# Attention by clusters, then a feed-forward block: routing two jobs ahead, maxima one job ahead

## The chip, the cores and the metric

The kernel runs on one core of a Trainium2 chip. The metric is the device time of one execution in microseconds (us). TensorE is PE in the profile (PEld is its weight load), VectorE is DVE, ScalarE is ACT, GpSimd is POOL, and SyncE, which issues all DMAs here, is SP.

## The reference

Queries, keys and values have 4 batches, 8 heads, 768 rows and 64 columns. Each query and each key goes to the nearest of 16 centroids of its head, and a query sees only the keys of its own centroid. The result feeds a block with two weight matrices.

```python
q_assign = argmax(q_n @ c_n.T)          # (B, H, S), 16 clusters; k_assign likewise
mask = q_assign[..., :, None] == k_assign[..., None, :]
scores = where(mask, (q @ k.T) / sqrt(64), -1e9)
attn = softmax(scores)                  # row maximum taken off first
x = (attn @ v) -> (3072, 512)           # heads side by side
h = x @ w_in                            # 512 x 2048
g = h * erf(log(1 + exp(h)))
out = g @ w_out                         # 2048 x 512
```

The weights arrive as 64-bit floats.

## The kernel before, in words

**Jobs.** Heads are taken in pairs, 16 pairs in all, 4 to a batch. A job is a pair and the query halves (384 columns each) that it computes. Jobs 0 to 3 take the first half of pairs 0 to 3, jobs 4 to 7 the second half, and jobs 8 to 19 both halves of pairs 4 to 15. A job has 6 units for each half: in a unit, `scores(u)` writes one key block against one half of both heads into PSUM (`sc`, lines 388 and 394), and ACT takes the exponent (`pr`, line 399). POOL adds the exponents up in `acc` (lines 403 and 407). `attend` multiplies them with the values (`av`, line 418), sums `acc` over the rows (`psum`, line 425), takes the reciprocal (`den`, line 430) and writes `xT` (line 439).

**What a job needs first.** `route(i)` transposes the query and key halves (`pt`, line 255), copies them to `qT` and `kT` (lines 262 and 264) and, crosswise, to the bf16 operands `qm` and `km` (lines 268 and 270), multiplies with the centroids (`psim`, line 276), copies to `sims` (line 283), transposes back (line 287), finds the nearest centroid (`mx`, `sims`, `mr`, `aq`, `ak`, lines 294 to 311), and transposes the one-hot masks (`pb`, line 321) into `qm` and `km` (lines 330 and 332). `shift(i)` then multiplies masks (`sm`, line 346) and lets DVE take the row maxima (`nmx`, line 350). They are joined (`nm`, line 355), transposed (`pn`, line 360), copied (`nmT`, line 362), written to DRAM (`line`, line 364) and read back as one row of `qm` (line 367). The second matmul of each score (line 394) needs that row.

`aside(i + 1)` runs `route` and then `shift` of the next job, one step of it in each slot of the current job; a job with one half has 24 slots, one with two halves 30. So one chain of work for one job runs beside the scores of the job before.

**Beside it.** `convert()` turns the 32 weight pieces from 64-bit to 32-bit floats, with two buffers: `fetch` (line 161), two ACT steps (lines 178 and 179), DVE steps on lines 180, 189, 194 and 197, POOL on line 200 and DVE's finish on line 166. `ffn_stream()` is the feed-forward block, cut into 12 chunks of 256 rows: `hidden` (`hp`, line 479), its copy (`g`, line 486), `gate` (lines 458 to 462) and `project` (`po`, line 500, and `osb`, line 507). `pump` hands out its matmuls by a budget in each slot. A chunk can start when `attend` has finished its rows in all four pairs of the batch.

**Buffers.** `qT`, `kT`, `qm` and `km` have two buffers each, the loaded `in_q` and `in_k` one. All of `pt`, `psim`, `pb`, `pn` and `psum` share a single PSUM buffer (pool `ps_t`). `sc` and `sm` share two (`ps_s`), `hp` and `po` two (`ps_f`), and `av` has one.

**Order.** The text above is not the order on the engines. A scheduler takes the recorded instructions, with their dependences and their buffers, and fixes a sequence for each engine when the program is built; each engine then runs its own sequence in order, waiting on semaphores.

Of the kernel before, what the change touches and what calls it, by code (L numbers as in the profile page):

```python
# [8 lines left out]
F32 = mybir.dt.float32  # L9
# [38 lines left out]
def kernel(  # L48
# [15 lines left out]
    const = pool("const", 1)  # L64
    stage = pool("stage", 1)
    vp = pool("vp", 2)
    rowp = pool("rowp", 2)
    routep = pool("routep", 1)
# [4 lines left out]
    gp = pool("gp", 2)  # L73
    outp = pool("outp", 2)
    setup = pool("setup", 1)
    linep = pool("linep", 2, space=bass.MemoryType.DRAM)
# [20 lines left out]

    def load(i, nm, src, pl, js=range(NJ)):
        if i >= len(JOBS):
            return  # L100
        p = JOBS[i][0]
        b, h0 = p // HP, 2 * (p % HP)
        t = pl.tile([P, NJ, 2, D], F32, name="in_" + nm)
        for e in range(2):
            nc.sync.dma_start(
                out=t[:, js[0] : js[-1] + 1, e],
                in_=src[b, h0 + e].rearrange("(p j) d -> p j d", p=P)[:, js[0] : js[-1] + 1],
            )
        work.setdefault(i, {})[nm] = t

    def chunks(i):

        halves = JOBS[i][1]
        return range(halves[0] * HJ, (halves[-1] + 1) * HJ)

    def load_qk(i):
        if i < len(JOBS):
            load(i, "q", q, stage, chunks(i))
            load(i, "k", k, stage)

    cen = setup.tile([P, D], F32, name="cen")
    nc.sync.dma_start(out=cen, in_=centroids.rearrange("h c d -> (h c) d"))
    load_qk(0)

# [81 lines left out]

    cn = setup.tile([P, 2, D], F32, name="cn")
    sq = cn[:, 0]
    ss = setup.tile([P, 1], F32, name="ss")
    nc.vector.tensor_tensor(out=sq, in0=cen, in1=cen, op=ALU.mult)  # L210
    nc.vector.reduce_sum(out=ss, in_=sq, axis=AX.X)
    nc.vector.tensor_scalar_max(out=ss, in0=ss, scalar1=1e-30)
    norm = setup.tile([P, 1], F32, name="norm0")
    nc.scalar.sqrt(norm, ss)
    for it in range(2):
        inv = setup.tile([P, 1], F32, name=f"inv{it}")
        nc.vector.reciprocal(out=inv, in_=norm)
        twice = setup.tile([P, 1], F32, name=f"twice{it}")
        nc.vector.scalar_tensor_tensor(
            out=twice, in0=ss, scalar=inv, in1=norm, op0=ALU.mult, op1=ALU.add  # L220
        )
        norm = setup.tile([P, 1], F32, name=f"norm{it + 1}")
        nc.vector.tensor_scalar(
            out=norm, in0=twice, scalar1=0.5, scalar2=(1e-6 if it else 0.0),
            op0=ALU.mult, op1=ALU.add,
        )
    rden = setup.tile([P, 1], F32, name="rden")
    nc.vector.reciprocal(out=rden, in_=norm)
# [15 lines left out]
    def route(i):  # L244
        p, halves = JOBS[i]
        st = work[i]
        parts = [("q", h) for h in halves] + [("k", h) for h in range(2)]
        for nm in "qk":
            st[nm + "T"] = rowp.tile([P, S], F32, name=nm + "T")

            st[nm + "m"] = rowp.tile([P, 2, S], BF16, name=nm + "m")
        for nm, half in parts:
            pt = ps_t.tile([P, HJ, P], F32, name="pt", tag="t")
            for jj in range(HJ):
                nc.tensor.transpose(  # L255
                    out=pt[:, jj], in_=st[nm][:, HJ * half + jj].rearrange("p e d -> p (e d)"),
                    identity=ident,
                )
            cols = slice(half * HW, (half + 1) * HW)
            raw = st[nm + "T"][:, cols]  # L260
            if nm == "q":
                nc.scalar.mul(out=raw, in_=pt.rearrange("p j t -> p (j t)"), mul=D**-0.5)
            else:
                nc.scalar.copy(out=raw, in_=pt.rearrange("p j t -> p (j t)"))
            for e in range(2):
                dst = st[nm + "m"][(1 - e) * D : (2 - e) * D, e, cols]
                if nm == "q":
                    nc.gpsimd.tensor_copy(out=dst, in_=raw[e * D : (e + 1) * D])
                else:
                    nc.scalar.copy(out=dst, in_=raw[e * D : (e + 1) * D])  # L270
            yield
        del st["q"], st["k"]
        load_qk(i + 1)
        psim = ps_t.tile([P, HW], F32, name="psim", tag="t")
        for g, (nm, half) in enumerate(parts):
            nc.tensor.matmul(  # L276
                psim[2 * C * g : 2 * C * (g + 1)], lhsT=ccT[:, p % HP],
                rhs=st[nm + "T"][:, half * HW : (half + 1) * HW],
                start=True, stop=True,
            )  # L280
        n = 2 * len(parts)
        sims = routep.tile([P, HW], F32, name="sims")
# [34 lines left out]

        for nm, src, js in (("qm", aq, chunks(i)), ("km", ak, range(NJ))):
            pb = ps_t.tile([P, NJ, P], BF16, name="pb", tag="t")
            for j in js:  # L320
                nc.tensor.transpose(  # L321
                    out=pb[:, j], in_=src[:, j % HJ, j // HJ].rearrange("p e c -> p (e c)"),
                    identity=identb,
                )
            cols = slice(js[0] * P, (js[-1] + 1) * P)
            for e in range(2):
                r = slice(e * D, (e + 1) * D)
                src = pb[r].rearrange("p j t -> p (j t)")[:, cols]
                if nm == "qm":
                    nc.vector.tensor_scalar_mul(out=st[nm][r, e, cols], in0=src, scalar1=-BIG)  # L330
                else:
                    nc.scalar.copy(out=st[nm][r, e, cols], in_=src)  # L332
            yield
# [3 lines left out]
    def shift(i):  # L337
        st = work[i]
        ts = chunks(i)
        n = len(ts)  # L340
        nmx = small.tile([P, NJ, 2, 2], F32, name="nmx")
        for t in ts:
            for half in range(2):
                sm = ps_s.tile([P, 2, 512], F32, name="sm", tag="s")
                for e in range(2):
                    nc.tensor.matmul(  # L346
                        sm[:, e, 0:HW], lhsT=st["qm"][:, e, t * P : (t + 1) * P],
                        rhs=st["km"][:, e, half * HW : (half + 1) * HW], start=True, stop=True,
                    )
# [14 lines left out]
        nc.sync.dma_start(out=line[0 : 2 * n], in_=nmT[0 : 2 * n])  # L364
        for e in range(2):
            r = e * D + SH
            nc.sync.dma_start(
                out=st["qm"][r : r + 1, e, ts[0] * P : (ts[-1] + 1) * P],
                in_=line[e * n : (e + 1) * n].rearrange("(o t) p -> o (t p)", o=1),
            )  # L370
        load(i, "v", v, vp)
        yield

# [7 lines left out]
    def scores(u):  # L381
        i, half, j = units[u]
        st = work[i]
        sc = ps_s.tile([P, 2, 512], F32, name="sc", tag="s")
        cols = slice(half * HW, (half + 1) * HW)
        for e in range(2):
            r = slice(e * D, (e + 1) * D)
            nc.tensor.matmul(  # L388
                sc[:, e, 0:HW], lhsT=st["kT"][r, j * P : (j + 1) * P], rhs=st["qT"][r, cols],
                start=True, stop=False,  # L390
            )
        for e in range(2):
            r = slice(e * D, (e + 1) * D)
            nc.tensor.matmul(  # L394
                sc[:, e, 0:HW], lhsT=st["km"][r, e, j * P : (j + 1) * P], rhs=st["qm"][r, e, cols],
                start=False, stop=True,
            )
# [13 lines left out]
    def attend(u0):  # L411
# [12 lines left out]
        for e in range(2):  # L424
            nc.tensor.matmul(  # L425
                psum[e * D : (e + 1) * D], lhsT=ones, rhs=st["acc", half][:, e], start=True, stop=True
            )
        den = routep.tile([P, HW], F32, name="den")
        nc.scalar.activation(out=den, in_=psum, func=ACT.Identity, bias=alleps)  # L429
        nc.vector.reciprocal(out=den, in_=den)  # L430
        x = xTs.setdefault(p, {})
        lo = half * HW
        while lo < (half + 1) * HW:
            c = lo // TB
            hi = min((c + 1) * TB, (half + 1) * HW)
            if c not in x:
                x[c] = xTp.tile([P, TB], F32, name=f"xT{c}", bufs=XBUFS[c])
            own = slice(lo - half * HW, hi - half * HW)
            nc.vector.scalar_tensor_tensor(  # L439
                out=x[c][:, lo - c * TB : hi - c * TB], in0=av[:, own], scalar=av[:, HW : HW + 1],  # L440
                in1=den[:, own], op0=ALU.add, op1=ALU.mult,
            )
# [103 lines left out]

    def aside(i):

        if i < len(JOBS):
            yield from route(i)  # L550
            yield from shift(i)

    conv = convert()
# [8 lines left out]

    for _ in aside(0):
        prepare(20)
    chunk_cost = NFT * HP * 4 * TB + TJ * NFT * 4 * DM
    ahead = iter(())
    for u in range(0, len(units), 2):
        i, half, j = units[u]
        p, halves = JOBS[i]
        if (half, j) == (halves[0], 0):  # L570
            ahead = aside(i + 1)
        scores(u)
# [8 lines left out]
        slots = SLOTS if len(halves) == 2 else 8  # L581
        for _ in range(slots):
            if part:
                pump(part * chunk_cost // (periods * slots) + 64)
            prepare(4 if i < HP else 6)
            next(ahead, None)
    attend(len(units) - NJ)
# [34 lines left out]
```

## Time and profile before

| | |
|---|---|
| runs | 1381.64, 1381.69 and 1383.28 us, median 1381.69 |
| profiled execution | 1381.38 us, of which its span is 1379.6 us (1.8 us lie around it) |
| granted TensorE clock, mean of the span | 0.956 |
| busy | PE 1265.8 us (92%), DVE 619.0 (45%), ACT 519.5 (38%), POOL 375.6 (27%) |
| first exponent of job 0 | at 47.32 us |
| jobs 0 to 3 | 47.32 to 197.21 us |
| jobs 4 to 7 | 197.21 to 347.31 us |
| jobs 8 to 19 | 347.31 to 1186.12 us |
| feed-forward block alone | 1186.12 to the end |

Job boundaries are put at the first exponent of each job. In rows of the profile "x" gives a count, the first number after the bar is busy time in us, the next the mean of one in ns, and what follows the second bar is idle time of the engine just before, with the engine and line that ended it.

### The profile page before, as it was taken

What the parts mean: (1) busy time and instruction counts of PE and PEld (TensorE: products, weight loads), DVE (VectorE), ACT (ScalarE), POOL (GpSimd) and SP (SyncE); (2) the same over time, 40 slices, a digit from 0 to 9 for tenths busy, and PEclk for the clock granted to TensorE, in tenths of its full rate; (3) what the DMA queues carried; (4) which work ended last, traced back from release to release, by engine and by line L of the source; (5) the groups of instructions that cost most, each with busy time, mean ns of one, the idle gap of its engine ahead of it and who ended that gap; (6) DMA issues with size and microseconds to landing.
All of it is one profiled execution on the core that took longest, in us unless ns stands there. A gap on an engine that the chain in (4) does not pass through costs nothing.

```text
span 1379.6 us, 13584 instructions
## 1 busy us (share of the span) xinstructions
PE 1265.8 (92%) x5393; PEld 667.9 (48%) x5393; DVE 619.0 (45%) x859; ACT 519.5 (38%) x645; POOL 375.6 (27%) x293
## 2 busy tenths in 40 slices
PE   3777768987999999999989999999999999999998
PEld 1222225532545544554644644644646546575764
DVE  6788777545335532724333353624342442221311
ACT  4444434642325423351442524423523524320311
POOL 2455434342323223232322133132322232100000
PEclk9877678998999999999999999999999999999999
DMA  4343322111101011010100101010100000000000
GB/s 134 98 116 90 92 83 67 29 41 40 24 10 41 12 23 42 8 36 8 31 12 8 43 1 46 5 42 9 35 8 8 12 9 8 0 16 8 8 16 15
DMA packets 96671, 46.09 MB, mean 33 GB/s; under 512 B 89400, under 2 KB 89440, under 8 KB 96608
## 3 DMA queue, kind: packets, MB, share of 16 engines
q1 hardware_dynamic: 96608, 45.23, 12.2%
q8 instruction: 42, 0.69, 0.2%
q14 instruction: 21, 0.17, 0.0%
HBM read 38.88 MB, written 6.34 MB: 33 GB/s over the span
## 4 chain that ended last, share of the span: by engine, by line
PE 69%; DVE 5%; ACT 5%; issue 3%; POOL 3%; DMA 0%; POOLq 0%; ACTq 0%; DVEq 0%
PE po L500 22%; PE hp L479 20%; PE av L418 9%; PE sc L388 9%; PE sm L346 4%; PE sc L394 2%; PE psum L425 1%; PE pt L255 1%; DVE nmx L350 1%; POOL acc L407 1%; ACT pr L399 1%; POOL sims L301 1%; PE pb L321 1%; ACT a_s L458 1%; PE psim L276 1%
## 5 line engine op out<-in xcount | busy, mean ns | idle before, releaser
L479 PE MATMUL hp<-xT,w_in 128*128 128x256 f32 x1536 | 383.4, 386 | 0.0
L500 PE MATMUL po<-w_out,g 128*128 128x512 f32 x768 | 372.8, 600 | 0.1
L407 POOL TENSOR_TENSOR acc<-acc,pr 128x768 f32<-128x768 f32 x128 | 220.6, 1724 | 473.2 <-ACT pr L399 460.6
L479 PEld LDWEIGHTS hp<-xT,w_in 128*128 128x128 f32 x1536 | 284.1, 191 | 105.0 <-issue 72.0
L399 ACT ACTIVATE pr<-sc 128x768 f32<-128x768 f32 x192 | 151.9, 810 | 265.5 <-PE sc L394 264.4
L350 DVE TENSOR_REDUCE nmx<-sm 128x2 f32<-128x768 f32 x192 | 179.4, 951 | 110.0 <-PE sm L346 108.6
L388 PE MATMUL sc<-qT,kT 64*128 64x384 f32 x768 | 203.7, 558 | 11.4 <-DVE nmx L350 5.8
L500 PEld LDWEIGHTS po<-w_out,g 128*128 128x128 f32 x768 | 138.8, 190 | 103.7 <-issue 91.2
L486 DVE COPY g<-hp 128x512 f32<-128x512 f32 x96 | 65.8, 686 | 238.3 <-PE hp L479 237.8
L418 PE MATMUL av<-pr,in_v 128*64 128x386 f32 x768 | 163.0, 516 | 0.2 <-DVE xT L439 0.2
L430 DVE RECIPROCAL den<-den 128x384 f32<-128x384 f32 x32 | 81.7, 2552 | 160.5 <-ACT den L429 160.5
L346 PE MATMUL sm<-km,qm 128*128 128x384 bf16 x384 | 106.3, 363 | 22.5 <-DVE nmx L350 14.7
L388 PEld LDWEIGHTS sc<-qT,kT 64*128 64x128 f32 x768 | 73.7, 200 | 93.4 <-issue 49.3
L458 ACT ACTIVATE a_s<-g 128x2048 f32<-128x2048 f32 x24 | 45.8, 1910 | 153.2 <-DVE g L486 147.4
L403 POOL TENSOR_TENSOR acc<-pr,pr 128x768 f32<-128x768 f32 x32 | 58.1, 1816 | 149.1 <-ACT pr L399 143.8
L418 PEld LDWEIGHTS av<-pr,in_v 128*64 128x64 f32 x768 | 55.3, 141 | 85.0 <-issue 79.4
L346 PEld LDWEIGHTS <-qm 128*128 128x128 bf16 x384 | 37.1, 103 | 105.6 <-issue 97.8
L462 DVE TENSOR_TENSOR g<-a_s,g 128x512 f32<-128x512 f32 x96 | 62.1, 702 | 44.8 <-ACT a_s L460 44.7
L394 PE MATMUL sc<-qm,km 64*128 64x384 bf16 x384 | 73.8, 343 | 5.7 <-DMA qm<-line 5.7
L332 ACT COPY km<-pb 64x768 bf16<-64x768 bf16 x40 | 31.7, 792 | 98.0 <-PE pb L321 97.4
L429 ACT ACTIVATE den<-psum,alleps 128x384 f32<-128x384 f32 x32 | 18.5, 579 | 120.6 <-PE psum L425 77.3
L200 POOL TENSOR_TENSOR a_s<-a_s 128x512 f32<-128x512 f32 x32 | 42.9, 1343 | 68.5 <-issue 35.3
(77 smaller groups left out, 823.1 us busy)
## 6 DMA issues: line engine op xcount, KB each, us to landing
a_s<-in_moe_w_in_dram SPq DMA_DIRECT2D x16, 512.0 KB
a_s<-in_moe_w_out_dram SPq DMA_DIRECT2D x16, 512.0 KB
in_k<-in_k_dram SPq DMA_DIRECT2D x40, 192.0 KB
in_v<-in_v_dram SPq DMA_DIRECT2D x40, 192.0 KB
out_dram<-osb SPq DMA_DIRECT2D x24, 256.0 KB
in_q<-in_q_dram SPq DMA_DIRECT2D x24, 192.0 KB
in_q<-in_q_dram SPq DMA_DIRECT2D x16, 96.0 KB
qm<-line SPq DMA_DIRECT2D x24, 1.5 KB
```

The source lines that it names most:

```text
L346: nc.tensor.matmul(sm[:, e, 0:HW], lhsT=st["qm"][:, e, t * P : (t + 1) * P], rhs=st["km"][:, e, half * HW : (half + 1) * HW], start=True, ...
L350: nc.vector.tensor_reduce(out=nmx[:, t, half], in_=sm[:, :, 0:HW], axis=AX.X, op=ALU.max, negate=True)
L388: nc.tensor.matmul(sc[:, e, 0:HW], lhsT=st["kT"][r, j * P : (j + 1) * P], rhs=st["qT"][r, cols], start=True, stop=False,)
L394: nc.tensor.matmul(sc[:, e, 0:HW], lhsT=st["km"][r, e, j * P : (j + 1) * P], rhs=st["qm"][r, e, cols], start=False, stop=True,)
L399: nc.scalar.activation(out=pr[:, :, 0:HW], in_=sc[:, :, 0:HW], func=ACT.Exp)
L407: nc.gpsimd.tensor_tensor(out=st["acc", half], in0=st["acc", half], in1=pr[:, :, 0:HW], op=ALU.add)
L418: nc.tensor.matmul(av[e * D : (e + 1) * D], lhsT=st["v"][:, j, e], rhs=prs[(u0 + j) % NPT][:, e], start=(j == 0), stop=(j == NJ - 1),)
L430: nc.vector.reciprocal(out=den, in_=den)
L462: nc.vector.tensor_tensor(out=h[:, i : i + GW], in0=s[i // half][:, i % half : i % half + GW], in1=h[:, i : i + GW], op=ALU.mult,)
L479: nc.tensor.matmul(hp[:, a], lhsT=w_in[:, r, f0 : f0 + P], rhs=xTs[b * HP + r][c], start=(r == 0), stop=(r == HP - 1),)
L486: nc.vector.tensor_copy(out=gs[n][:, fp * GW : (fp + 1) * GW], in_=hp)
L500: nc.tensor.matmul(po, lhsT=gs[n][:, ft, tt * P : (tt + 1) * P], rhs=w_out[:, ft], start=(ft == 0), stop=(ft == NFT - 1),)
```

## The change

The loads come by halves into three buffers that queries and keys share (`in_qk`), and each transposed part draws the next load. `kT` and `km` have three buffers; `qT` and `qm` are cut into halves with four buffers. `route` and `shift` become two sequences that take alternate slots: during job i, `shift` runs for job i + 1 and `route` for job i + 2, and what is left of both is issued at the end of the job. Before the first score, `route(0)`, `shift(0)` and `route(1)` are issued. The row of maxima is read back by halves. `den` goes: the sum plus its constant is written into `xT`, and its reciprocal is taken there, in pieces that follow the 256-row chunks. `osb` has one buffer instead of two, and the tiles of the setup lie in the last `pr` buffer.

```diff
-    stage = pool("stage", 1)
+    stage = pool("stage", 3)
-    rowp = pool("rowp", 2)
+    rowp = pool("rowp", 3)
-    outp = pool("outp", 2)
-    setup = pool("setup", 1)
+    outp = pool("outp", 1)
...
+    def load_parts():
+
+        for i, (p, _) in enumerate(JOBS):
+            for nm, h in parts(i):
+                src = q if nm == "q" else k
+                work.setdefault(i, {})[nm, h] = load(stage, "in_qk", src, p, range(h * HJ, (h + 1) * HJ))
+                yield
...
-        for nm in "qk":
-            st[nm + "T"] = rowp.tile([P, S], F32, name=nm + "T")
-
-            st[nm + "m"] = rowp.tile([P, 2, S], BF16, name=nm + "m")
+        st["kT"] = rowp.tile([P, S], F32, name="kT")
+
+        st["km"] = rowp.tile([P, 2, S], BF16, name="km")
+        for h in halves:
+            st["qT", h] = rowp.tile([P, HW], F32, name="qT", bufs=4)
+            st["qm", h] = rowp.tile([P, 2, HW], BF16, name="qm", bufs=4)
...
             for jj in range(HJ):
                 nc.tensor.transpose(
...
+                    out=pt[:, jj], in_=src[:, jj].rearrange("p e d -> p (e d)"), identity=ident
                 )
+            next(loads, None)
...
-        del st["q"], st["k"]
-        load_qk(i + 1)
...
+                if nm == "q":
+                    for h in hs:
+                        nc.vector.tensor_scalar_mul(
+                            out=st["qm", h][r, e], in0=pb[r, h].rearrange("p j t -> p (j t)"), scalar1=-BIG
+                        )
...
+        for m, h in enumerate(halves):
+            for e in range(2):
+                r = e * D + SH
+                t0 = e * n + m * HJ
+                nc.sync.dma_start(
+                    out=st["qm", h][r : r + 1, e],
+                    in_=line[t0 : t0 + HJ].rearrange("(o t) p -> o (t p)", o=1),
+                )
...
-        den = routep.tile([P, HW], F32, name="den")
-        nc.scalar.activation(out=den, in_=psum, func=ACT.Identity, bias=alleps)
-        nc.vector.reciprocal(out=den, in_=den)
...
+            dst = x[c][:, lo - c * TB : hi - c * TB]
+            nc.scalar.activation(out=dst, in_=psum[:, own], func=ACT.Identity, bias=alleps)
+            nc.vector.reciprocal(out=dst, in_=dst)
...
-    for _ in aside(0):
+
+    def ahead(fn, i):
+        return fn(i) if i < len(JOBS) else iter(())
+
+    for _ in route(0):
         prepare(20)
+    routing = route(1)
+    for _ in shift(0):
+        prepare(20)
+        next(routing, None)
+    for _ in routing:
+        pass
...
-            ahead = aside(i + 1)
+            shifting, routing = ahead(shift, i + 1), ahead(route, i + 2)
...
-            next(ahead, None)
+            n = slots * (halves.index(half) * HJ + j // 2) + slot
+            next((shifting, routing)[n % 2], None)
+        if (half, j) == (halves[-1], NJ - 2):
+            for rest in (shifting, routing):
+                for _ in rest:
+                    pass
```

## The prediction

> **What bounds the kernel now.** I read the page first (PE busy 92%), then busy time by stage, since a share of the whole span hides stages with different limits. Columns: stretch, its length, then busy us (and instructions) of PE, PEld, DVE, ACT, POOL; granted TensorE clock; DMA share; GB/s. The rows are jobs 0 to 3, 4 to 7, 8 to 19, and the tail.
>
> ```profile
> 47.32:197.21 149.89, 108.00 (x404) 40.77 (x405) 123.31 (x167) 65.47 (x104) 70.09 (x49) 0.72 0.32 91
> 197.21:347.31 150.10, 127.19 (x585) 60.75 (x584) 89.73 (x120) 70.21 (x101) 56.00 (x46) 0.90 0.20 51
> 347.31:1186.12 838.81, 818.97 (x3710) 442.22 (x3710) 337.83 (x435) 323.25 (x381) 234.46 (x170) 1.00 0.08 20
> 1186.12:1379.60 193.48, 189.66 (x631) 115.61 (x629) 38.84 (x57) 38.89 (x25) 1.68 (x1) 1.00 0.03 11
> ```
>
> From job 8 on PE is busy for 1008.6 of 1032.3 us at full clock: only 23.7 us of idle time can go there, and any new wait of PE costs its whole length. In jobs 0 to 3 it is otherwise: DVE is busiest (123.3 of 149.9 us, 82%), PE idles for 42 us and its clock is 0.72. The waits of PE in that stage say on whom:
>
> ```profile
> PE pb L321 <- DVE aq L311: 8.1, 4, 3.5
> PE sm L346 <- DVE nmx L350: 7.9, 10, 1.6
> PE pb L321 <- DVE qm L330: 4.3, 3, 2.2
> PE sm L346 <- ACT km L332: 3.5, 4, 0.9
> PE sc L394 <- DMA qm<-line: 2.8, 1, 2.8
> ```
>
> Almost all are links of `route` and `shift`. The timeline of DVE and PE in job 1 shows how: six maxima in one run, with PE between them waiting, and no conversion in DVE for 5.5 us.
>
> ```profile
> 107.28 5.51 DVE L350 TENSOR_REDUCE nmx<-sm 128x2 f32<-128x768 f32 x6
> 108.29 1.66 PE L346 MATMUL sm<-km,qm 128*128 128x384 bf16 x4 [1.44 <-DVE nmx L350]
> ```
>
> Last, what fills DVE there (groups by line, same stage):
>
> ```profile
> L197 DVE SCALAR_TENSOR_TENSOR a_s<-a_s 128x512 f32<-128x512 uint32 x21 | 23.3, 1115 | 0.3
> L189 DVE SCALAR_TENSOR_TENSOR a_s<-a_s 128x512 uint32<-128x512 uint32 x21 | 17.6, 842 | 2.5 <-ACT a_s L179 2.1
> L194 DVE TENSOR_SCALAR a_s<-a_s 128x512 uint32<-128x512 uint32 x21 | 14.1, 675 | 0.3
> L180 DVE TENSOR_SCALAR a_s<-a_s 128x512 uint32<-128x512 uint32 x20 | 11.1, 554 | 3.0 <-DMA a_s<-in_moe_w_in_dram 1.5 <-DMA a_s<-in_moe_w_out_dram 1.3
> ```
>
> With L166 (21.7 us for 19) the conversion takes 87.8 of the 123.3 us. Attention alone would leave DVE more than half free.
>
> **Step 1, the early jobs.** No matmul is added or removed (3337 in both programs); the order changes. In the built programs I counted what stands on DVE ahead of `nm` of job 4. Before: 25 finishes of a weight piece (L166) and 101 other conversion instructions; after: 21 and 85. Pieces move behind attention, because attention, no longer one chain, gets ahead of them. That is 4 x 1.14 + 16 x 0.80 (mean of the four rows) = 17.4 us of DVE work. `nm` of job 4 ends DVE's first 191.0 us, 149.1 of them busy (78%); (149.1 - 17.4) / 0.78 = 169 us, 22 us earlier. Bounds: +6 if DVE does not set the pace (ahead of job 0's `nm` stand one finish and four other conversion steps more, 4.3 us, and `route(1)`'s small reductions, about 1.9 us); -45 if DVE, better fed, is 90% busy (131.7 / 0.9 = 146 us). I take -22, the proportion being nearest to the rows.
>
> **Step 2, what comes back.** The four pieces now run between `nm` of jobs 5 and 7 (231 to 301 us before). There DVE was busy 41.5 of 69.7 us and PE 59.8, so 17.4 us fit beside PE. I take +2, between 0 and 17.4; the cover is PE's feed-forward matmuls.
>
> **Step 3, the query buffers.** Four half buffers hold two full jobs. From job 8 on, `route(i + 2)` can't copy its second query half until job i has made its last score. That `pt` meanwhile keeps the only `ps_t` buffer, so `psum` and `pn` queue behind it. The built order shows it: the two key parts, `psim`, `pb`, both `psum` and the next job's `pn` stand together at each job's end, and the scores' second matmul (L394 before) waits behind all. The chain, from rows: query copy 0.6; two key parts, each 1.12 (the `pt` at 343.25, 344.38 and 345.50); `psim` to the end of `km` in job 8, 315.59 to 325.04 = 9.4; a reciprocal and `xT` that DVE's new order puts in between, 2.55 + 0.75 = 3.3; `pn` to the score, where the DMA was waited for:
>
> ```profile
> 340.70 0.22 PE L360 MATMUL pn<-identb,nm 128*12 128x128 bf16 x1 [0.18 <-DVE nm L355]
> ...
> 345.98 0.49 PE L394 MATMUL sc<-qm,km 64*128 64x384 bf16 x2
> ```
>
> = 5.3. Sum 20.8 us; 17.5 where no reciprocal comes between, 26 if two links wait as `pb` does at worst elsewhere (2.8 and 2.2). PE loses what its own order does not cover. I add up its matmuls between the last score of a job and the first completed one of the next, at steady prices: busy time by instruction of the program, of which an fp32 one has two rows in the trace (`hp` 383.4/768 = 0.50, `po` 372.8/384 = 0.97; from 600 to 1180 us `av` 0.37, a score 0.46 + 0.17, small ones 0.1 to 0.5). Jobs 8, 10, 12, 14 and 16 end with 24 to 26 us, job 9 with 30, 13 and 17 with 47 and more: covered, half of it by the feed-forward block; I take 2 for all eight (6 if the chain takes 26). Jobs 11 and 15 end with 16.8 us, at the change of batch where little feed-forward work is ready: 4.0 each. Job 7 ends with 11.3 against 17.5: 6.2, less the 2.9 us that PE idles in 335.00 to 347.31 before: 3.3. Sum +13 (5 with a chain of 17.5, 33 with one of 26).
>
> **Step 4, edits that cost nothing.** ACT's 32 row sums become 64 pieces (each about half of 0.58 us) and DVE's 32 reciprocals 64 pieces of the same total; 24 more `qm` copies of 0.35 us take the place of wider ones. All lie beside PE from job 8 on. Five of 76 ACT table loads (1.28 us) go, also beside PE. One `osb` buffer suffices: two `po` are 16 x 0.97 = 15.5 us apart. If that cover went, 24 stores would wait; I see no place. SP issues 64 more loads (0.38 to 0.54 us) and 24 more reads of `line` (0.215): 30 to 40 us of SP over the whole span. SP runs in order, so a load that waits for its buffer holds weight fetches, `line` and `qm` behind it, as it does before; no wait of PE on `in_q` or `in_k` stands among the waits, so 0; at worst three more waits of 2.8.
>
> The Trainium skill, page "DMA: Bandwidth & Descriptors", sections "Anatomy of one DMA" and "Bandwidth", speaks against cutting loads: it asks for 1 MiB or more and gives some 2.0 us fixed for each, fitted on another issue path. Its 88 x 2.0 = 176 us would be an estimate for transfers that are waited for one by one; the waits here show only `qm`.
>
> In jobs 0 to 3 the row has a clock of 0.72, with one PE wait of 3.5 us and the others shorter, so I count nothing for shorter gaps. The Trainium skill, page "TensorE: Matmul & The Clock Gate", Part 1, lets PE's clock halve only after an idle window of about 3.4 us. By it gaps kept below that length would give full clock, an estimate of 30 us of PE time in that stage; the row, with gaps that are nearly all shorter and a clock of 0.72, does not agree.
>
> **Sum.** -22 + 2 + 13 = -7: 1381.4 (span 1379.6 and 1.8 around it) becomes 1374.5; the median of the runs, 1381.7, is the same within the 0.2% (2.8 us) that a measurement of this kernel can tell.
>
> **Rivals.** *The query buffers decide.* The chain is longer than I make it, since ACT and DVE run in order and have evictions and gates between its links. At 28 us the five ends with 24 to 26 us lose 16 together, jobs 11 and 15 11.2 each, job 7 10.5: -22 + 2 + 49 = +29, 1410; at 25 us 2 + 16 + 8, so +6, 1387. It decides from about 24 us on, and I price it at 1397, between the two. For it: one `ps_t` buffer for five users, and no wait for the row from job 9 on before. Against: the feed-forward work that stands in the gaps. *The clock comes back.* If the early jobs keep PE warm, 108.0 x 0.28 = 30 us of PE time go and DVE rises to 90%: -45 + 2 + 13 = -30, 1351. For it: waits of the routing chain are most of PE's gaps. Against: DVE still sets the pace. *Nothing moves.* Step 1 brings 15 us and the job ends cost as much: 1381.
>
> **How the numbers follow.** Forecast 0.45 (own range 1362 to 1379), clock 0.12, nothing 0.08, buffers 0.35. Range 1348 to 1402, which leaves out the outer parts of the first and last rival. Faster 0.56 (forecast and clock, less a little), same 0.09, slower 0.35.
>
> **What would show it.** Right: job 8 starts near 330 us; jobs 0 to 3 shorter than 150 us with fewer weight pieces converted in them; waits of `sm` on `nmx` gone; new PE waits at the ends of jobs 7, 11 and 15 on `pb`, `pn` or `qm`. Wrong: an early stage as long as before, or waits of 3 us and more at most job ends from job 8 on.

## Result: slower by one per cent, and the profile after

The changed kernel takes 1396.35 us (median of 4, 1392.58 to 1397.32) where the kernel before takes 1381.66 in the same comparison: ratio 1.010, 95% interval 1.0079 to 1.0121. The profiled execution took 1396.29, its span 1394.5.

Busy time by stage, jobs 0 to 3, 4 to 7, 8 to 19 and the tail, in the kernel after (columns as in the prediction):

```profile
50.51:183.96 133.45, 102.91 (x418) 38.02 (x419) 102.66 (x147) 62.24 (x103) 63.68 (x47) 0.81 0.31 89
183.96:346.73 162.77, 132.09 (x588) 67.27 (x588) 103.68 (x148) 69.39 (x106) 57.73 (x45) 0.82 0.21 57
346.73:1201.04 854.31, 832.77 (x3677) 444.88 (x3678) 327.64 (x471) 319.06 (x397) 232.85 (x169) 0.98 0.07 19
1201.04:1394.60 193.56, 189.66 (x631) 115.61 (x629) 38.66 (x58) 39.05 (x27) 2.69 (x2) 1.00 0.03 11
```

The early gain is there: jobs 0 to 3 are 16.4 us shorter (133.45 for 149.89), less 3.2 us of a longer prologue. Jobs 4 to 7 give it back (+12.7), so job 8 starts at 346.73, 0.6 us earlier than before; jobs 8 to 19 then lose 15.5 us at a clock of 0.98.

These are waits of PE in jobs 0 to 3 after. The waits of `sm` on `nmx`, ten with 7.9 us before, are down to one; those of `sc` on `nmx` have grown from 2.7 us to 9.0, and those of `pb` on `qm` from 4.3 to 6.1:

```profile
PE sc L407 <- DVE nmx L368: 9.0, 4, 3.3
PE pb L337 <- DVE qm L345: 6.1, 2, 4.5
PE sm L364 <- DVE nmx L368: 1.7, 1, 1.7
```

The end of job 11 follows, from PE's timeline. The last score of job 11 ends at 580.4 us, the first finished score of job 12 (`sc<-qm,km`) starts at 610.58, and between them the links of `route(13)` and of job 12's `pn` stand one behind another:

```profile
585.86 0.90 PE L273 MATMUL pt<-ident,in_qk 128*128 128x128 f32 x3 [1.74 <-ACT kT L281]
...
591.66 0.90 PE L302 MATMUL pt<-ident,sims 128*128 128x128 f32 x3 [0.60 <-ACT sims L298]
593.97 1.55 PE L444 MATMUL psum<-acc,ones 128*64 128x384 f32 x4 [1.40 <-DVE sims L312]
596.34 0.80 PE L337 MATMUL pb<-identb,aq 128*128 128x128 bf16 x6 [0.82 <-ACT xT L456]
599.04 3.78 PE L497 MATMUL hp<-xT,w_in 128*128 128x256 f32 x8 [1.91 <-DVE xT L458]
...
604.99 0.22 PE L378 MATMUL pn<-identb,nm 128*12 128x128 bf16 x1
...
610.58 0.49 PE L413 MATMUL sc<-qm,km 64*128 64x384 bf16 x2
```

`psum` and `pb` come through the one small PSUM buffer between the links of the routing. No wait is over 1.91 us, but the granted clock (the third figure from the end) falls to a half between 584 and 588 and stays there until after 602:

```profile
580.00:584.00 4.00, 3.96 (x17) 1.96 (x13) 0.00 (x0) 3.96 (x5) 1.96 (x2) 1.00 0.01 2
584.00:588.00 4.00, 1.04 (x6) 0.52 (x5) 2.50 (x4) 3.95 (x5) 0.72 (x2) 0.74 0.23 53
588.00:592.00 4.00, 3.40 (x14) 1.02 (x15) 0.00 (x0) 2.84 (x6) 1.67 (x1) 0.50 0.21 48
...
600.00:604.00 4.00, 4.00 (x17) 3.14 (x16) 0.62 (x3) 0.68 (x1) 0.00 (x0) 0.63 0.00 0
```

Job 11 as a whole has 8.3 us of idle PE and a clock of 0.87 (before 3.4 and 1.00), job 15 6.9 us and 0.93 (before 1.0 and 1.00). In jobs 8 to 19 together PE's idle time grows by only 1.7 us (21.5 for 19.8) and its busy time by 13.8.

### The profile page after: what moved, and what is told of

The parts are those of the page before. It is cut to its first block, busy times and chain, and to the rows that moved or that the text cites. A ratio compares the mean times of both kernels' runs of the same rounds, so it can differ in the third digit from the quotient of the medians.

```text
span 1394.5 us, 13869 instructions
## 1 busy us (share of the span) xinstructions
PE 1278.3 (92%) x5393; PEld 675.0 (48%) x5393; DVE 608.7 (44%) x915; ACT 514.7 (37%) x672; POOL 374.3 (27%) x293
## 4 chain that ended last, share of the span: by engine, by line
PE 78%; DVE 8%; ACT 6%; issue 3%; POOL 2%; DMA 1%; SPq 0%; ACTq 0%; POOLq 0%; DVEq 0%
PE po L518 24%; PE hp L497 23%; PE av L437 10%; PE sc L407 9%; PE sm L364 4%; PE sc L413 2%; ACT pr L418 2%; PE pt L273 2%; PE psum L444 1%; PE pb L337 1%; DVE xT L457 1%; DVE nmx L368 1%; PE psim L291 1%; ACT L418 1%; POOL a_s L202 1%
## 5 line engine op out<-in xcount | busy, mean ns | idle before, releaser
L497 PE MATMUL hp<-xT,w_in 128*128 128x256 f32 x1536 | 395.9, 393 | 7.8 <-DVE xT L458 7.8
L497 PEld LDWEIGHTS hp<-xT,w_in 128*128 128x128 f32 x1536 | 289.4, 195 | 125.0 <-issue 82.2
L407 PE MATMUL sc<-qT,kT 64*128 64x384 f32 x768 | 200.1, 547 | 18.0 <-DVE nmx L368 13.6
L437 PE MATMUL av<-pr,in_v 128*64 128x386 f32 x768 | 172.2, 521 | 2.3 <-DVE xT L458 2.2
L457 DVE RECIPROCAL xT<-xT 128x256 f32<-128x256 f32 (+1 forms) x64 | 82.9, 1328 | 98.1 <-ACT xT L456 98.0
L364 PE MATMUL sm<-km,qm 128*128 128x384 bf16 x384 | 95.9, 337 | 14.0 <-ACT pr L418 10.2
L413 PE MATMUL sc<-qm,km 64*128 64x384 bf16 x384 | 70.0, 336 | 0.0
L456 ACT ACTIVATE xT<-psum,alleps 128x256 f32<-128x256 f32 (+1 forms) x64 | 24.0, 417 | 114.7 <-PE psum L444 79.8
L273 PE MATMUL pt<-ident,in_qk 128*128 128x128 f32 x216 | 44.2, 319 | 21.0 <-ACT xT L456 6.8
```

The lines of the kernel that those rows point to most:

```text
L273: nc.tensor.transpose(out=pt[:, jj], in_=src[:, jj].rearrange("p e d -> p (e d)"), identity=ident)
L364: nc.tensor.matmul(sm[:, e, 0:HW], lhsT=st["qm", t // HJ][:, e, t % HJ * P : (t % HJ + 1) * P], rhs=st["km"][:, e, half * HW : (half + 1) ...
L407: nc.tensor.matmul(sc[:, e, 0:HW], lhsT=st["kT"][r, j * P : (j + 1) * P], rhs=st["qT", half][r], start=True, stop=False,)
L413: nc.tensor.matmul(sc[:, e, 0:HW], lhsT=st["km"][r, e, j * P : (j + 1) * P], rhs=st["qm", half][r, e], start=False, stop=True,)
L437: nc.tensor.matmul(av[e * D : (e + 1) * D], lhsT=st["v"][:, j, e], rhs=prs[(u0 + j) % NPT][:, e], start=(j == 0), stop=(j == NJ - 1),)
L457: nc.vector.reciprocal(out=dst, in_=dst)
```

## The experiments

Three theories stood first: A, the query buffers; B, the conversion that is deferred to jobs 4 to 7; and C, the small edits. All ratios are to the kernel before, run on the same chip.

### One job ahead again: from job 8 on, and throughout

`one_late`:

```diff
-            shifting, routing = ahead(shift, i + 1), ahead(route, i + 2)
+            shifting = ahead(shift, i + 1) if i < 8 else aside(i + 1)
+            routing = ahead(route, i + 2) if i < 7 else iter(())
...
-            next((shifting, routing)[n % 2], None)
+            next((shifting, routing)[n % 2] if i < 8 else shifting, None)
```

Here `aside(i)` is `route(i)` and then `shift(i)`, as in the kernel before.

> Routing two ahead up to the routing of job 8, from job 8 on route and then shift of the next job in one sequence as before; loads by halves, buffers, denominators as in the changed kernel. Theory A (four query half buffers make the end of a full job a serial chain, PE waits there at the ends of jobs 11 and 15, and its clock falls behind the waits): jobs 8 to 19 go from 854.3 back to about 839 us, jobs 11 and 15 idle under 3.5 us at a clock of 1.00, total 1396.3 - 15.5 = 1381 (1377 to 1385). Theory C (the small edits cost it: loads by halves in SP's queue, one buffer for the output, denominators in pieces): jobs 8 to 19 stay near 854, total 1396 (1392 to 1400).

`one_all` has `shifting = aside(i + 1)` in every job, and `aside(0)` before the loop.

> Route and shift as one sequence one job ahead throughout, as before the change, with everything else of the change kept. Theories A and B (what counts is the order of route and shift: at the job ends of the full jobs, and in the early jobs): the time of before, 1382 (1378 to 1386), jobs 0 to 3 near 150 us and jobs 4 to 7 near 150 us. Theory C (the small edits): 1396 (1391 to 1400), with 8 to 19 near 854.

Measured: `one_late` 1409.9 us (1.020, 1.018 to 1.022), `one_all` 1420.4 (1.027, 1.025 to 1.029). All three missed: the old order with the new small edits is 37 us slower than the old kernel, and slower than the changed one. Most of the loss lies in jobs 11 and 15, each with 11.5 us of idle PE in both kernels. One number was of use: up to job 7 `one_late` has a free buffer for every query half that it routes (job 7 itself routes nothing), and its job 8 starts at 331.2 us, 16.1 earlier than before.

### Six query halves, and a faster conversion

`q6`:

```diff
-            st["qT", h] = rowp.tile([P, HW], F32, name="qT", bufs=4)
-            st["qm", h] = rowp.tile([P, 2, HW], BF16, name="qm", bufs=4)
+            st["qT", h] = rowp.tile([P, HW], F32, name="qT", bufs=6)
+            st["qm", h] = rowp.tile([P, 2, HW], BF16, name="qm", bufs=6)
...
```

> The changed kernel with six query half buffers of each kind in place of four. To make room the last four rows of the second weight share one tile, so the feed-forward part reads wrong weights there; instructions, shapes and sizes are unchanged. Theory A: the copies of the query halves of job i + 2 wait for no score of job i, the chain leaves the job ends, jobs 11 and 15 lose 12 us of length together, jobs 8 to 19 near 840, total 1383 (1379 to 1387). Rival A' (the chain is long because of the one small PSUM buffer and the in-order queues of ScalarE and VectorE, whatever the query buffers): jobs 11 and 15 keep their 5 to 7 us of idle PE, total 1393 to 1397. Theory C: 1396.

Measured: 1359.7 us (0.983, 0.981 to 0.985), 36.7 less than the changed kernel and faster than the kernel before. Its jobs 4 to 7 and 8 to 19:

```profile
180.69:332.52 151.83, 127.64 (x590) 65.20 (x589) 102.39 (x148) 70.88 (x108) 59.97 (x49) 0.88 0.23 61
332.52:1160.49 827.97, 813.86 (x3676) 444.46 (x3676) 330.93 (x471) 317.52 (x392) 231.81 (x165) 0.99 0.08 19
```

Jobs 8 to 19 become 26.3 us shorter, more than A had said, and job 7 falls from 41.8 to 34.7. Job 11 keeps 0.8 us of idle PE, at full clock. A is right in kind but 23 us short; A' is out by its total and by job 11. Job 15 still idles PE for 4.6 us at a clock of 0.92, which `q6_den` below takes away (1.3 and 1.00).

`pace6`:

```diff
-            prepare(4 if i < HP else 6)
+            prepare(6)
```

> The changed kernel with the weight conversion paced at 0.6 of a step a slot in jobs 0 to 3 too, in place of 0.4. Theory B (the gain of jobs 0 to 3 is deferred conversion, and it is paid back in jobs 4 to 7 wherever the steps stand): jobs 0 to 3 get longer by about what jobs 4 to 7 get shorter, job 8 starts near 347, total 1396 (1393 to 1399). Rival B' (the deferred steps cost more in jobs 4 to 7 than they save before, because ScalarE waits there for the weight's load ahead of PE's work): job 8 starts 5 to 13 us earlier, total 1383 to 1391.

Measured: 1399.0 us (1.011, 1.009 to 1.013). Jobs 0 to 3 take 153.9 us (+20.5), jobs 4 to 7 149.7 (-13.1): conversion taken earlier is paid earlier, with 7.4 us more than it saves. B' is out: ScalarE's waits for weight loads in jobs 4 to 7 fall from 21.2 to 5.8 us, and job 8 starts no earlier. B's total holds at its edge, its start of job 8 does not (354.1 for 347).

### The denominators in pieces

The 37 us of `one_all` needed a cause. `b_den` is the kernel before with the change's edit of `den` alone:

```diff
-        den = routep.tile([P, HW], F32, name="den")
-        nc.scalar.activation(out=den, in_=psum, func=ACT.Identity, bias=alleps)
-        nc.vector.reciprocal(out=den, in_=den)
...
+            nc.scalar.activation(out=dst, in_=psum[:, own], func=ACT.Identity, bias=alleps)
+            nc.vector.reciprocal(out=dst, in_=dst)
...
```

> The kernel before with one edit of the change alone: the sums of a row of queries go straight into the pieces of xT and are inverted there, and the tile den is gone. The one-ahead order with all the small edits took 1420 where the kernel before takes 1383, 38 us that no step of mine priced; they lie in jobs 11 and 15 (15 and 20 us) and in jobs 13 with 14 and 17 with 18 (5 each). Theory D (the denominators in pieces): 1410 to 1422 here, with 11 us of idle PE in jobs 11 and 15. Theory L (the loads by halves and the split of query operands): 1381 to 1386 here, as before.

`one_all_den`, `a_den` and `q6_den` are the reverse, the tile `den` put back into the one-ahead order, the changed kernel and the kernel with six halves.

> Route and shift one job ahead throughout with the small edits of the change, but with den as a tile of its own again; the last two rows of the second weight share one tile to make room, so those products read wrong weights, at unchanged order, shapes and sizes. Theory D: 1380 to 1386, the time of before. Theory L: 1414 to 1422, as without den.

> The changed kernel with den as a tile of its own again (last two rows of the second weight share one tile, as above). Theory D as a cost of its own that the changed order also pays: 1358 to 1370. Theory D': the edit hurts only in the one-ahead order, and the changed kernel's loss is that of the query buffers: 1391 to 1400. Theory L: 1396.

> Six query half buffers of each kind and den as a tile of its own (the last five rows of the second weight share one tile). With six buffers alone the changed kernel takes 1360. Theory D: 1340 to 1352, since jobs 14 and 15 with six buffers still idle PE for 3.0 and 4.6 us and run below full clock; Theory D': 1355 to 1362.

Measured medians, with the runs from above:

| order, query halves | den apart | den in pieces |
|---|---|---|
| before's code, one ahead | 1383.1 | 1429.7 (`b_den`; 1.033, 1.032 to 1.035) |
| the change's code, one ahead, four | 1385.1 (`one_all_den`; 1.001, 1.0005 to 1.002) | 1420.4 |
| two ahead, four | 1395.0 (`a_den`; 1.009, 1.007 to 1.010) | 1396.4, the change |
| two ahead, six | 1338.7 (`q6_den`; 0.968, 0.967 to 0.969) | 1359.7 |

D holds in three rows: 47, 35 and 21 us, though `b_den` lies 8 us above the range that was given for it and `q6_den` 1 us below. In the changed kernel itself the edit costs 1.4 us, within the spread of its runs, as D' said; but with six halves it costs 21, so D' does not hold for the two-ahead order as such. `a_den` still idles PE for 8.6 and 9.3 us in jobs 11 and 15, so the query halves alone hold the routing there; that the two stalls lie over each other is the reading that fits the four rows. `one_all_den` shows that loads by halves, query operands in halves and one output buffer together cost 2 us in the one-ahead order, so L is out, and of C only the denominators are left.

What the edit does is in ScalarE's timeline at the head of job 11. Before, the sum goes to `den` and the routing starts:

```profile
540.31 0.58 ACT L429 ACTIVATE den<-psum,alleps 128x384 f32<-128x384 f32 x1 [3.17 <-PE psum L425]
542.12 0.49 ACT L262 ACTIVATE qT<-pt 128x384 f32<-128x384 f32 x1 [1.22 <-PE pt L255]
```

In `b_den` the sum's second piece must wait for a buffer of `xT` that feed-forward matmuls still read; `psum` meanwhile keeps the small PSUM buffer, and `pt` stands behind it:

```profile
543.77 0.37 ACT L437 ACTIVATE xT<-psum,alleps 128x128 f32<-128x128 f32 x1 [3.16 <-PE psum L425]
...
564.94 0.47 ACT L437 ACTIVATE xT<-psum,alleps 128x256 f32<-128x256 f32 x1 [7.57 <-PE hp L478]
566.13 0.49 ACT L262 ACTIVATE qT<-pt 128x384 f32<-128x384 f32 x1 [0.72 <-PE pt L255]
```

The routing of job 12 starts 27 us into job 11 (566.13 less the first exponent at 539.01) for 6.6 before. Meanwhile PE has run its feed-forward work in one piece,

```profile
552.22 13.54 PE L478 MATMUL hp<-xT,w_in 128*128 128x256 f32 x62
```

and little is left to cover the routing chain later in the job. PE idles for 11.3 us, and its clock in that job is 0.85:

```profile
539.01:619.66 80.65, 69.36 (x304) 38.06 (x301) 31.61 (x44) 32.42 (x38) 20.05 (x15) 0.85 0.08 19
```

The direct test gives `b_den` more buffers of `xT`:

```diff
-XBUFS = (5, 5, 6)
+XBUFS = (8, 8, 8)
...
```

> The kernel before with the denominators in pieces, as in the run that took 1430, and eight buffers for each piece of xT in place of 5, 5 and 6 (the last five rows of the second weight share one tile to make room; its products read wrong weights, at unchanged shapes and sizes). Theory D1 (writing the sums into xT makes ScalarE wait for a buffer of xT that feed-forward matmuls still read, 7.6 us at the head of job 11, while psum keeps the only small PSUM buffer and the routing behind it): the wait goes, jobs 11 and 15 lose their 11 us of idle PE, total 1375 to 1390. Theory D2 (two short reciprocals and sums in place of one long one, or ScalarE's order, cost it): 1420 to 1432.

Measured: 1386.3 us (1.001, 1.000 to 1.003). ScalarE no longer waits for `hp` in job 11, which takes 65.86 us again at full clock, with 4.4 us of idle PE (3.4 before). D1 is shown; D2 is out. What eight buffers would do for the kernel before itself was not run.

### A version that has the room

`q6_den` takes its room from the second weight. `fit` finds it with all weights kept; its `den` is a plane of `acc` that only `psum`'s matmuls still had to read, and `operands` is the first part of `shift`, one job ahead:

```diff
-            st["qT", h] = rowp.tile([P, HW], F32, name="qT", bufs=4)
-            st["qm", h] = rowp.tile([P, 2, HW], BF16, name="qm", bufs=4)
+            st["qT", h] = rowp.tile([P, HW], F32, name="qT", bufs=6)
...
+    def operands(i):
...
+        st["km"] = rowp.tile([P, 2, S], BF16, name="km", bufs=2)
+        for h in halves:
+            st["qm", h] = rowp.tile([P, 2, HW], BF16, name="qm", bufs=4)
...
     def shift(i):
+        yield from operands(i)
...
+        den = st["acc", half][:, 0]
+        nc.scalar.activation(out=den, in_=psum, func=ACT.Identity, bias=alleps)
+        nc.vector.reciprocal(out=den, in_=den)
...
```

> A whole version that fits: the changed kernel with den kept in the plane of acc that the row sums have just read, and route cut after its maxima; the operands of the bias (qm, km and their transposes) are made one job ahead, at the head of shift, so that km needs two buffers and qm four, and the room of the third km buffer goes to six qT halves. Slots alternate as in the change. Theory A with D (what the change lacks is room for the raw query halves and for den): 1338 to 1352, as with six buffers and den apart (1339). Rival: the transposes of aq and ak, now at the head of each job ahead of its maxima, are a chain of their own there: 1360 to 1385.

`fit3` is `fit` with other slots:

```diff
-            next((shifting, routing)[n % 2], None)
+            next(routing if n % 3 == 2 else shifting, None)
```

> As the last one, with two slots of three for the operands and maxima of the next job and one of three for the routing two ahead, since the first sequence is now 15 steps of a full job's 30 and the second 5. Theory A with D: 1335 to 1352. Rival: 1360 to 1385.

Measured: `fit` 1376.5 us (0.995, 0.994 to 0.997), inside the rival's range; `fit3` 1350.1 (0.976, 0.974 to 0.977), inside A's. Here the sequence with the shorter lead needed the denser slots, and that one line is worth 26 us. `fit3` beats both kernels, by 2.4% and 3.3%. Its jobs 0 to 3, 4 to 7 and 8 to 19:

```profile
57.05:200.37 143.32, 102.39 (x406) 39.17 (x405) 112.44 (x152) 63.26 (x96) 68.11 (x49) 0.80 0.33 92
200.37:351.50 151.13, 120.07 (x588) 62.96 (x587) 92.79 (x130) 68.58 (x89) 52.21 (x42) 0.89 0.19 48
351.50:1158.93 807.43, 797.40 (x3688) 441.44 (x3688) 325.39 (x448) 318.67 (x357) 235.47 (x169) 1.00 0.08 20
```

Its gain is all in the full jobs, 31.4 us below before. Its job 8 starts 4.2 us later than before: the prologue is 9.7 us longer (57.05 us, and 59.01 in `fit`), and jobs 4 to 7 take 9.6 us longer than in `fit` (151.1 for 141.6). No run shows why.

## Why the prediction was wrong

The forecast was 1374.5 and faster; the kernel takes 1396.35 and is slower. The rival *the query buffers decide* named the mechanism that came: the chain of `route(i + 2)` at the end of a full job, bare where little feed-forward work is ready. That its price of 1397 is met so closely is luck. Its five ends in jobs 8, 10, 12, 14 and 16, put at 16 us together, show 0.0 to 1.2 us of idle PE each, and the early gain it counted did not last: job 8 starts at 346.73, where the first sign of being right was a start near 330.

- **Step 1, the early jobs: right in kind, a little large.** It said -22 at `nm` of job 4. There `nm` ends at 173.25 us for 191.12, so -17.9, and job 4's first exponent comes 13.2 us earlier (16.5 in `q6`); all lie within the bounds. DVE finishes 16 weight pieces in jobs 0 to 3 for 19 (L168 after, L166 before), and PE's idle time falls from 41.9 to 30.5 us.
- **Step 2, what comes back: not settled.** It said +2. Where every query half of that stage has a free buffer, jobs 4 to 7 take 150.8 us (`one_late`) and 151.8 (`q6`) for 150.1, which agrees. In `q6_den` they take 161.1, after 126.5 for jobs 0 to 3, and job 8 starts only 9.5 us earlier than before; no run shows why. Of the 10.9 us by which jobs 4 to 7 are longer in the changed kernel than in `q6`, 7.1 are job 7 alone (41.8 for 34.7), and that is step 3. For the other 4 us no cause was shown, and the runs of `q6` spread over 6.5 us.
- **Step 3, the query buffers: the term that failed.** It said +13. With six halves the change is 36.7 us faster, and 56.3 with `den` apart (1395.0 less 1338.7). Three sizes were short. The chain is about 28 us at the end of job 11, from the `pt` at 582.73 to the score at 610.58, for 20.8 and a bound of 26: the rows it was added up from are a link's time alone, and here ScalarE and VectorE bring `xT`'s sums and reciprocals and PE its own order between the links, at half the clock for much of the way. Job 7 lost 7.1 us, and 8.6 with `den` apart (44.0 in `a_den` for 35.4 in `q6_den`), for 3.3. And the idle time that was counted (4.0 for each of jobs 11 and 15; 4.9 and 5.9 measured) was not all: the clock fell behind it, which was counted as nothing, and costs, as an estimate from the rows' busy time and clock, 58.59 x 0.13 = 7.6 us in job 11 and 67.67 x 0.07 = 4.7 in job 15. These three do not make up the whole: of the 26.3 us by which `q6` shortens jobs 8 to 19, idle time is 7.4 and busy time 18.9, of which the clock is about 7 by the same estimate. The other 12 belong to the open point below.
- **Step 4, edits that cost nothing: wrong for `den`, right for the rest.** The pieces were counted as work, of which there is hardly more. What changed is the destination: the row sums leave PSUM only when a buffer of `xT` is free. That is 47 us in the order of before and 21 in the change with room, and hidden in the change as built. Loads, output buffer and halves cost 2 us, as said. The Trainium skill, page "DMA: Bandwidth & Descriptors", section "Bandwidth", asks for transfers of 1 MiB or more, for at least 75% of peak bandwidth. The change goes the other way with 64 more and smaller loads, and whatever they cost is within those 2 us.
- **What no step had.** With room, the two-ahead order takes 32.5 us off jobs 8 to 19 (838.8 to 806.3 in `q6_den`). "Only 23.7 us of idle time can go there" was read as a ceiling; but idle time fell by only 9.9 us, and PE's busy time by 22.7 at nearly the same number of records (3710 and 3673, one job's routing fewer). So busy time was no floor. Over the whole run the same 768 records of `av` take 163.0 us before and 151.6 in `q6_den`:

```profile
L418 PE MATMUL av<-pr,in_v 128*64 128x386 f32 x768 | 163.0, 516 | 0.2 <-DVE xT L439 0.2
```

```profile
L437 PE MATMUL av<-pr,in_v 128*64 128x386 f32 x768 | 151.6, 506 | 0.1
```

Part of that is the clock of the early jobs. The larger part is not: in jobs 8 to 19, at a clock of 1.00 in both, 552 of these records take 104.5 us before and 97.6 in `q6_den`, with a mean of 495 and 492 ns for one, so they overlap more. Why they pack more densely in the new order is open.

So the order of the change, with room, is worth -44 us (1338.7 for 1383.1) where it was put at -20. In the profiled executions 9.5 us of it lie ahead of job 8, where all 20 were looked for, and 32.5 in the full jobs, where none were. Its missing room costs +56 where it was put at +13. Each was too small by more than a half, and their sum changed sign. In jobs 8 to 19 the measured +15.5 stands near the 10 that step 3 had there, but that too is luck: the changed kernel is 48.0 us longer there than `q6_den`, and the 32.5 that no step had hide most of it.

## What to carry to other kernels

Before work is moved a job ahead, count the buffers of every operand that it writes: if the last copy must wait for the job in hand, the lead is lost at the job's end, and a chain that shares one PSUM buffer with other users takes them along. An eviction from PSUM is costed by when its destination comes free, not by its own length: in `b_den` 0.47 us of work came 21 us after its first piece. A scratch tile can be worth more than the memory that leaving it out saves; in `fit` a plane that its only reader had just left served as one. When a step of the right kind gives the wrong sign, put back one edit at a time in both orders, since two stalls on the same buffer can hide each other.

## What the runs showed of the hardware

The clock fell to a half after one short wait. In the kernel after, PE was busy for 13.92 of the 14 us ahead of 584, waited for 1.74 us up to 585.86, and the clock was at 1.00 until 585.5 and at 0.50 from 586. The waits of 0.60 to 1.91 us that follow came when it was down already:

```profile
584.00:585.50 1.50, 0.12 (x1) 0.00 (x0) 0.03 (x1) 1.50 (x2) 0.72 (x2) 1.00 0.56 128
585.50:586.00 0.50, 0.14 (x1) 0.14 (x2) 0.50 (x1) 0.48 (x2) 0.00 (x0) 0.88 0.05 10
```

It was at 1.00 again from 603, after PE had been busy without a break from 599.04. A longer wait did not do it: in the kernel before, a wait of 2.76 us left the clock at 1.00, as PE's row and the stretch around it show.

```profile
704.17 0.51 PE L321 MATMUL pb<-identb,aq 128*128 128x128 bf16 x6 [2.76 <-DVE aq L311]
700.00:708.00 8.00, 5.24 (x25) 2.59 (x24) 2.29 (x5) 1.15 (x2) 3.06 (x3) 1.00 0.01 2
```

So the length of a single wait does not decide, and what does was not measured. The Trainium skill, page "TensorE: Matmul & The Clock Gate", Part 1, has the clock follow recent activity and drop after an idle window of about 3.4 us. The rows agree with the first; against the second, a wait of about half that length was enough in one place.
